# Attention and feed-forward on one core: loads held to 800 KB under way, pooled scores as four products on two banks, and a band mask built for one block and spread by VectorE

## The chip, the core and the metric

The kernel runs on one core of a Trainium2 chip. The metric is the device time of one execution in microseconds. Three timed runs of the kernel before gave 1001.52, 1004.47 and 1006.77 us, so its time is 1004.47 us (the median). The profile that is read here is of one more execution, which took 1000.71 us.

## What is computed

There are 8 batches, 8 heads, 576 tokens and a head size of 64. Each head runs two attentions over the same inputs, and their sum goes through a feed-forward layer:

```python
q_d = q.reshape(B, H, Sd, factor, D).mean(axis=3)      # k_d, v_d likewise; factor = 4, Sd = 144
out_up = np.repeat(sm_attn(q_d, k_d, v_d), factor, axis=2)
mask = np.abs(pos[:, None] - pos[None, :]) < factor
scores = np.where(mask, scale * np.matmul(q, k.transpose(0, 1, 3, 2)), -1000000000.0)
out_local = np.matmul(softmax(scores), v)
x = out_up + out_local                                  # tokens x 512
h = x @ w_in                                            # 512 -> 2048
out = (h * np.cos(h)) @ w_out                           # 2048 -> 512
```

The *pooled* attention works on 144 queries and 144 keys per head; the *local* one on a band of seven keys around each query.

## The kernel before

**Units.** The attention is cut into 32 units, one for each batch b and pair of heads. The two heads of a pair lie on partitions 0 to 63 and 64 to 127. A unit has these steps: `u_qk` loads q and k (292 KB each) and sums four neighbouring columns into `qkd`; `u_v` loads the value blocks `vl` (384 KB); `u_vd` loads (288 KB, batches 0 and 1 alone) and sums the pooled values, as `v_sum` does for the later batches; `u_s` makes the scores and the softmax of both attentions; `u_t` transposes the weights; `u_pv` multiplies by the values and writes x in two f16 parts.

**Local scores.** The 576 tokens are cut into 24 segments of 24 queries, each with 32 keys. Twelve blocks (`NBLK`) of 32 columns hold them: 48 products of 32x32 (L643) fill 384 columns of one PSUM bank `bl`. For batches 0 and 1 (`early`) the band mask is first put into the bank by a product of the bf16 identity with `mask_b` (L637), and VectorE takes the row maximum and subtracts it (L666, L667). Later batches add the f32 `mask` on VectorE (L670).

**Pooled scores.** The 144 queries of a head are cut into three overlapping groups of at most 64, so that the two heads stand on the two halves of the partitions: six products of 64 queries by 144 keys (L652) fill 432 columns of a second bank `bp`. VectorE takes the row maxima (L673), ScalarE the three exponentials (L681). The weights `smd` (128 x 3 x 144) are transposed in `u_t`, per half of the keys, by two transposes of 128 columns (L714) and one product of 32 columns (L716).

**Constants.** GpSimd builds the two identities, then the mask over all twelve blocks: a memset (L348), eight band selections of 32 partitions x 384 columns (L351, L353), four memsets for the edges (L356, L357) and a bf16 copy (L358).

**Feed-forward.** x is cut into 12 tiles of 384 tokens and the 2048 hidden columns into 16 chunks. One step, of 192, is `gemm1` (12 products of 128x384, L811), the evaluation of h cos h on ScalarE and VectorE, and `gemm2` (9 products of 128x512, L850). The first three tiles go through the chunks in blocks, while the weights are still arriving; later tiles take all 16 chunks at once. The weights come as 32 loads of 512 KB into a ring of seven buffers `wd`, which the loads of `u_vd` and `v_norm` share, and are split into f16 parts on VectorE and ScalarE (`w_split`). Partial results of the first three tiles are added in memory by GpSimd's transfers (L876); first parts and whole results are stored from SyncE's queue (L873).

**What sets the order.** All operations are recorded with an engine, a cost and their buffers in a `Plan`; `schedule` orders them by list scheduling over these costs, and the program is written out in that order, so each engine and SyncE's queue of transfers run it strictly in sequence. In gaps that the plan expects on TensorE in the first 300 us, filler products of the identity are put (L988), 16 of them ahead of the first unit. Loads of batches 0 and 1 and the weights are chained in one fixed sequence. Transfers from SyncE carry eight semaphores in turn, so that a ninth one waits for the first.

Of the kernel before, what the change touches and what calls it, by code (L numbers as in the profile page):

```python
# [12 lines left out]
F32 = mybir.dt.float32  # L13
I32 = mybir.dt.int32
BF16 = mybir.dt.bfloat16
F16 = mybir.dt.float16
AF = mybir.ActivationFunctionType
ALU = mybir.AluOpType
AX = mybir.AxisListType
# [5 lines left out]
P = 128  # L25
# [12 lines left out]
SD = S // 4  # L38
# [5 lines left out]
PAD = 3  # L44
SP_ = S + 8
NBLK = 2 * NSEG
QG = 64
NQG = -(-SD // QG)
F64_TOP = float(np.uint32(0x47EFFFFF).view(np.float32))
NEG = -2.0 ** 100  # L50
NEARLY = 2
# [2 lines left out]
GRP = 2  # L54
HOLD = 6
NWD = 7
EARLY = {0: dict(s="pa.0 pa.1 po.0 po.1", t="pa.2", v="ph.0 ph.1"),
         1: dict(s="pa.0 pa.1 po.0 po.1", t="pa.2 po.2", v="ph.0 ph.1 pa.0 pa.1 ph.0 ph.1 po.0 po.1")}
BOOST = {0: 100.0, 1: 30.0}
# [237 lines left out]
def _act(n, psum=True, extra=0):  # L297
    return n * 0.000833 + (0.051 if psum else 0.093) + 0.093 * extra


def _dve(n):
    return n * 0.001042 + 0.065
# [11 lines left out]
def attn_ffn_kernel(ctx: ExitStack, tc: tile.TileContext, qT, kT, vdn, vl, w_in, w_out, out):  # L314
# [21 lines left out]
    ident_b, ident = const.tile([P, P], BF16, name="ident_b"), const.tile([P, P], F32, name="ident")  # L336
    bquart, bhalf = const.tile([P, 1], F32, name="bquart"), const.tile([P, 1], F32, name="bhalf")
    ones, tiny = const.tile([P, P], F32, name="ones"), const.tile([P, P], F32, name="tiny")
    mask, mask_b = const.tile([P, NBLK, BS], F32, name="mask"), const.tile([P, NBLK, BS], BF16, name="mask_b")

    def constants():
        make_identity(nc, ident_b)
        make_identity(nc, ident)
        dve.memset(bquart, -0.25)
        dve.memset(bhalf, -0.5 * PI)
        dve.memset(ones, 1.0)
        dve.memset(tiny, TINY)
        pool.memset(mask, 0.0)  # L348
        for i in range(4):
            h = mask[i * BS:(i + 1) * BS]  # L350
            pool.affine_select(out=h, in_=h, compare_op=ALU.is_ge, fill=NEG, base=0,  # L351
                               pattern=[[0, NBLK], [1, BS]], channel_multiplier=-1)
            pool.affine_select(out=h, in_=h, compare_op=ALU.is_ge, fill=NEG, base=2 * PAD,  # L353
                               pattern=[[0, NBLK], [-1, BS]], channel_multiplier=1)
        for h in range(2):
            pool.memset(mask[2 * BS * h:2 * BS * h + BS, 0, 0:PAD], NEG)  # L356
            pool.memset(mask[2 * BS * h + BS:2 * BS * h + 2 * BS, NBLK - 1, BQ + PAD:BS], NEG)  # L357
        pool.tensor_copy(mask_b, mask)  # L358

# [13 lines left out]
    w_dram = {"i": w_in.bitcast(I32).rearrange("(a p) (f t) -> p a f t", p=P, t=2),  # L375
              "o": w_out.bitcast(I32).rearrange("f (n t) -> f n t", t=2)}

    loads = {}

    def dma(nbytes, fn, r=(), w=(), pw=()):  # L380
        o = pl.op("SP", max(0.45, nbytes / 262e3), fn, r=r, w=w, pw=pw, lat=1.8)
        loads.setdefault((pl.name,) + pl.arg, []).append(o)
        return o

# [168 lines left out]
    def bank(b, kind):  # L553

        if b < NEARLY:
            tags = EARLY[b][kind].split()
            return psum(tags[int(pl.turn(f"early{b}{kind}", len(tags)).split(".")[-1])])
        return psum(pl.turn("pa", 3))
# [63 lines left out]
    def u_s(b, pr):  # L622
        pl.name = "u_s"
        u = st[(b, pr)]
        q, k, qkd, qkg = u["q"], u["k"], u["qkd"], u["qkg"]
        early = b < NEARLY
        sml, smd = ub(b, pr, "sml"), ub(b, pr, "smd")
        bl, bp = bank(b, "s"), bank(b, "s")
        loc, poo = pl.buf(None), pl.buf(None)

        def using(bk, o):
            bk.r.append(o)
            bk.acc.append(o)

        def l_mm():
            if early:
                pe.matmul(bl.get()[:, :NBLK * BS], ident_b, mask_b.rearrange("p s n -> p (s n)"), start=True, stop=False)  # L637
            for a in range(NSEG // 2):
                for i in range(4):
                    for e in range(2):  # L640
                        for h in range(2):
                            hs, o, c, w = slice(64 * h, 64 * h + 64), (8 * a + 4 * e + i) * BQ, 4 * a + i, 2 * h + e
                            pe.matmul(bl.get()[BS * w:BS * (w + 1), BS * c:BS * (c + 1)], q.get()[hs, o:o + BS], k.get()[hs, o:o + BS],  # L643
                                      start=not early, stop=not early or c == NBLK - 1)
        if early:
            pl.op("PE", 1.2, l_mm, r=[q, k], pw=[bl], w=[loc])

        def d_mm():
            for g in range(NQG):
                for h in range(2):  # L650
                    hs, o = slice(64 * h, 64 * h + 64), min(g * QG, SD - QG)
                    pe.matmul(bp.get()[hs, g * SD:(g + 1) * SD], qkg()[hs, 0, o:o + QG], qkg()[hs, 1, :],  # L652
                              start=True, stop=True)
        if early:
            pl.op("PE", 0.6, d_mm, r=[qkd], pw=[bp], w=[poo])
        else:
            pl.op("PE", 1.5, lambda: (l_mm(), d_mm()), r=[q, k, qkd], pw=[bl, bp], w=[loc, poo])

        n, m = NBLK * BS, NQG * SD
        mxl, mxd, su = sb("mxl", 2, [P, NBLK]), sb("mxd", 2, [P, NQG]), sb("su", 2, [P, NBLK + NQG])  # L660
        sul, sud = lambda: su.get()[:, :NBLK], lambda: su.get()[:, NBLK:]
        lq = lambda: bl.get()[:, :n].rearrange("p (c n) -> p c n", n=BS)
        dq = lambda: bp.get()[:, :m].rearrange("p (g n) -> p g n", g=NQG)
        wide = lambda t, size: t.unsqueeze(2).broadcast_to([P, t.shape[1], size])
        if early:
            using(bl, pl.op("DVE", _dve(n), lambda: dve.tensor_reduce(out=mxl.get(), in_=lq(), axis=AX.X, op=ALU.max), r=[loc], w=[mxl]))  # L666
            using(bl, pl.op("DVE", _dve(n), lambda: dve.tensor_tensor(out=sml.get(), in0=lq(), in1=wide(mxl.get(), BS), op=ALU.subtract),  # L667
                            r=[loc, mxl], w=[sml]))
        else:
            using(bl, pl.op("DVE", _dve(n), lambda: dve.tensor_tensor(out=sml.get(), in0=lq(), in1=mask, op=ALU.add), r=[loc], w=[sml]))  # L670
            pl.op("DVE", _dve(n), lambda: dve.tensor_reduce(out=mxl.get(), in_=sml.get(), axis=AX.X, op=ALU.max), r=[sml], w=[mxl])
            sub(n, sml.get, sml.get, lambda: wide(mxl.get(), BS), r=[mxl], w=[sml])
        using(bp, pl.op("DVE", _dve(m), lambda: dve.tensor_reduce(out=mxd.get(), in_=dq(), axis=AX.X, op=ALU.max, negate=True),  # L673
                        r=[poo], w=[mxd]))
        part = pl.buf(None)

        def exps():
            act.activation(mxd.get(), mxd.get(), AF.Copy, scale=1.0 / 128.0)
            act.activation(sml.get(), sml.get(), AF.Exp, scale=0.125)
            for g in range(NQG):  # L680
                act.activation(smd.get()[:, g], dq()[:, g], AF.Exp, bias=mxd.get()[:, g:g + 1], scale=1.0 / 128.0,  # L681
                               accum_out=sud()[:, g:g + 1])
        using(bp, pl.op("ACT", _act(n, False) + 1.2, exps, r=[poo], w=[mxd, sml, smd], pw=[su, part], tab="exp"))
        pl.op("DVE", _dve(n), lambda: dve.tensor_reduce(out=sul(), in_=sml.get(), axis=AX.X, op=ALU.add), r=[sml], pw=[su, part])
        g = b // GRP
        pl.op("DVE", 0.1, lambda: dve.tensor_scalar(out=su.get(), in0=su.get(), scalar1=1e-9, scalar2=xnorm[g].get() if g else 2.0 * PI,
# [13 lines left out]
    def u_t(b, pr):  # L700
        pl.name = "u_t"
        u = st[(b, pr)]
        sml, smd = u["sml"], u["smd"]
        ptd = ub(b, pr, "ptd")
        pl.op("DVE", _dve(NBLK * BS), lambda: dve.transpose(sml.get().rearrange("p c n -> p (c n)"), sml.get().rearrange("p c n -> p (c n)")),
              w=[sml])
        for kh in range(2):
            bk = bank(b, "t")

            def t_mm(kh=kh, bk=bk):  # L710
                ks = slice(kh * HD, (kh + 1) * HD)
                to = bk.get()[:HD, :2 * SD].rearrange("p (h n) -> p h n", h=2)
                for g in range(NQG - 1):
                    pe.transpose(to[:, :, g * QG:(g + 1) * QG], smd.get()[:, g, ks], ident)  # L714
                w = SD - (NQG - 1) * QG
                pe.matmul(to[:, :, SD - w:], smd.get()[:, NQG - 1, ks], ident.rearrange("p (h n) -> p h n", h=2)[:, :, QG - w:],  # L716
                          start=True, stop=True)
            pl.op("PE", 4 * 0.065, t_mm, r=[smd], w=[bk])
            evac(2 * SD, lambda kh=kh: ptd.get()[:, kh],
                 lambda bk=bk: bk.get()[:HD, :2 * SD].rearrange("p (a n) -> p a n", a=2), bk, ptd, scale=1.0)  # L720
        u["ptd"] = ptd
# [26 lines left out]
    def u_pv(b, pr):  # L748
# [22 lines left out]
                            pe.matmul(banks[e].get()[64 * h:64 * h + 64, o:o + BQ], vt.get()[r, a, i, :], sml.get()[r, 4 * a + i, :BQ],  # L771
                                      start=True, stop=True)
        if b < NEARLY:
            pl.op("PE", 1.52, l_mm, r=[vt, sml], pw=banks, w=loc)
        else:
            pl.op("PE", 2.16, lambda: (d_mm(), l_mm()), r=[vd, ptd, vt, sml], pw=banks, w=loc + [poo])

        evac(SD, xd.get, lambda: banks[0].get()[:, 2 * SD:3 * SD], banks[0], xd, scale=0.25)
        xd.w[-1].deps += poo.w
# [194 lines left out]
                        best = (max(x[1], t0), x[1], x[2])  # L974
        return best

    last = CFG["f0"]
    with tc.manual_schedule():
        constants()
        for o in order:  # L980
            if o.eng == "PE" and o.start < CFG["fend"]:
# [5 lines left out]
                for _ in range(max(n, CFG["warm"][o.arg[0]] if early and s else 0)):  # L987
                    pe.matmul(s[2].get()[:, :2 * P], ident_b, ident_b.unsqueeze(1).broadcast_to([P, 2, P]), start=True, stop=True)  # L988
                last = o.start + o.dur
            o.fn()  # L990


def _lay(inputs):
# [32 lines left out]
```

## Time and profile before

| | us |
|---|---|
| median of three timed runs | 1004.47 (1001.52 to 1006.77) |
| profiled execution | 1000.71 |
| its span, first to last instruction | 998.9 |
| TensorE busy | 956.5 (96%) |
| VectorE busy | 649.1 (65%) |
| ScalarE busy | 601.2 (60%) |
| GpSimd busy | 220.2 (22%) |
| granted TensorE clock, mean | 0.981 |

A row of a group gives line, engine, operation, output and inputs by tile name, shapes, count, busy time and the mean duration. A row of the timeline gives start, duration, the instruction with its count, and in brackets the idle time of the engine before it with what ended it. f32 products appear as two records each, so that 48 products count as x96. PE is TensorE's products, PEld its weight loads, DVE VectorE, ACT ScalarE, POOL GpSimd, SP SyncE.

### The profile page before, as it was taken

To read this page: it belongs to the slowest core of one execution; us is meant where nothing else is said; L and a number is where in the kernel's file an instruction comes from. 1 tells how busy PE (TensorE), PEld (TensorE's weight loads), DVE (VectorE), ACT (ScalarE), POOL (GpSimd) and SP (SyncE) were. 2 spreads that over 40 slices of the span, in tenths; PEclk is the share of its full clock that TensorE was granted. 3 is DMA by queue.
4 is the path that set the end of the run, shared out by engine and by line. 5 is a ranking of instruction groups with operands and counts; after the bars stand their busy time and mean duration, and the time that the engine had idled before them with its cause. 6 is when DMAs were issued, how large, how long until landed. Compare 5 with 4: busy or idle time off the path is not lost.

```text
span 998.9 us, 26495 instructions
## 1 busy us (share of the span) xinstructions
PE 956.5 (96%) x11333; PEld 558.1 (56%) x11333; DVE 649.1 (65%) x1272; ACT 601.2 (60%) x1225; POOL 220.2 (22%) x360
## 2 busy tenths in 40 slices
PE   7788889989999999999999999999999999999998
PEld 5566445545556655655555665655555665555554
DVE  5968979697878856745555764755555764544443
ACT  2736667677887655656465764656555764644543
POOL 4544823241443311301011320401010210000000
PEclk8979979999999999999999999999999999999999
DMA  8632896576645631321100530321010000000000
GB/s 243 242 124 86 231 270 166 111 168 186 151 85 109 149 78 41 81 57 42 46 27 25 129 90 9 91 63 41 34 41 25 19 34 1 2 32 1 32 1 32
DMA packets 41854, 84.81 MB, mean 85 GB/s; under 512 B 4040, under 2 KB 14536, under 8 KB 41736
## 3 DMA queue, kind: packets, MB, share of 16 engines
q1 hardware_dynamic: 35256, 69.15, 21.6%
q0 software_dynamic: 6480, 13.96, 9.5%
q8 instruction: 89, 1.46, 0.6%
q14 instruction: 29, 0.24, 0.1%
HBM read 65.01 MB, written 18.09 MB: 83 GB/s over the span
## 4 chain that ended last, share of the span: by engine, by line
PE 81%; DVE 6%; ACT 3%; issue 3%; DMA 3%; POOL 2%; POOLq 0%; ACTq 0%; DVEq 0%
PE bank L850 33%; PE bank L811 33%; PE bank L771 4%; PE bank L643 3%; PE bank L652 3%; PE bank L759 2%; PE bank L988 1%; PE bank L714 1%; DMA out<-ob 1%; DMA wd<-vdn 1%; DVE wv L427 1%; DVE tr L826 1%; DVE wv L429 1%; DMA wd<-w_in 1%; ACT wd L435 1%
## 5 line engine op out<-in xcount | busy, mean ns | idle before, releaser
L850 PE MATMUL bank<-wo,gh 128*128 128x512 f16 x1152 | 343.9, 380 | 8.6 <-ACT ob L867 7.3
L811 PEld LDWEIGHTS <-wi 128*128 128x128 f16 x2304 | 225.5, 99 | 178.6 <-issue 12.8
L850 PE MATMUL bank<-wo,gl 128*128 128x512 f16 x576 | 218.6, 380 | 1.4 <-POOL gl L387 1.1
L825 ACT ACTIVATE tr<-bank,bquart,hs 128x384 int32<-128x384 f32 x192 | 128.3, 669 | 108.5 <-PE bank L811 102.8
L826 DVE SCALAR_TENSOR_TENSOR tr<-bank,hs,tr 128x384 f32<-128x384 f32 x192 | 117.9, 615 | 115.3 <-ACT tr L825 114.9
L850 PEld LDWEIGHTS <-gh 128*128 128x128 f16 x1152 | 109.5, 99 | 117.8 <-issue 15.4
L829 DVE SCALAR_TENSOR_TENSOR tr<-tr,rho,bank 128x384 f32<-128x384 f32 x192 | 116.8, 609 | 83.1 <-ACT tr L828 82.8
L828 ACT ACTIVATE tr<-tr,bhalf 128x384 f32<-128x384 f32 x192 | 117.4, 613 | 79.5 <-DVE tr L826 78.5
L831 ACT ACTIVATE gh<-tr 128x384 f16<-128x384 f32 x181 | 94.4, 521 | 113.5 <-DVE tr L829 113.2
L387 DVE TENSOR_TENSOR gl<-tr,gh 128x384 f16<-128x384 f32 x170 | 95.6, 563 | 67.5 <-ACT gh L831 66.2
L811 PE MATMUL bank<-x0h,wi 128*128 128x384 f16 x384 | 103.6, 332 | 7.4 <-DVE tr L829 5.2
L811 PE MATMUL bank<-x1h,wi 128*128 128x384 f16 x384 | 102.9, 330 | 0.0
L811 PE MATMUL bank<-x2h,wi 128*128 128x384 f16 x384 | 101.5, 326 | 0.7 <-DVE tr L829 0.7
L811 PE MATMUL bank<-x3h,wi 128*128 128x384 f16 x384 | 101.5, 326 | 0.0
L850 PEld LDWEIGHTS <-gl 128*128 128x128 f16 x576 | 56.5, 98 | 70.7 <-POOL gl L387 1.6
L574 POOL TENSOR_TENSOR qkd<-q 128x144 f32<-128x144 f32 x25 | 14.6, 585 | 264.6 <-PE bank L652 260.8
L811 PE MATMUL bank<-x0l,wi 128*128 128x384 f16 x192 | 63.8, 332 | 0.0
L811 PE MATMUL bank<-x1l,wi 128*128 128x384 f16 x192 | 63.4, 330 | 0.0
L811 PE MATMUL bank<-x3l,wi 128*128 128x384 f16 x192 | 62.6, 326 | 0.0
L811 PE MATMUL bank<-x2l,wi 128*128 128x384 f16 x192 | 62.6, 326 | 0.0
L771 PE MATMUL bank<-sml,vl 32*64 32x24 f32 x3072 | 53.0, 214 | 1.2 <-issue 0.7
L771 PEld LDWEIGHTS bank<-sml,vl 32*64 32x64 f32 x3072 | 49.4, 135 | 8.0 <-issue 5.2
(155 smaller groups left out, 1208.7 us busy)
## 6 DMA issues: line engine op xcount, KB each, us to landing
vl<-vl SPq DMA_DIRECT2D x32, 384.0 KB, 3.5
q<-qT SPq DMA_DIRECT2D x32, 292.0 KB, 3.7
k<-kT SPq DMA_DIRECT2D x32, 292.0 KB, 4.0
out<-ob SPq DMA_DIRECT2D x36, 256.0 KB, 2.7
out<-ob POOLq DMA_DIRECT2D x33, 256.0 KB, 5.8
wd<-w_in SPq DMA_DIRECT2D x16, 512.0 KB, 4.5
wd<-w_out SPq DMA_DIRECT2D x16, 512.0 KB, 6.3
wd<-vdn SPq DMA_DIRECT2D x18, 384.0 KB, 4.4
```

The costliest lines, as they stand in the source:

```text
L387: f = lambda e: lambda: e.tensor_tensor(out=out(), in0=in0(), in1=in1(), op=ALU.subtract)
L643: pe.matmul(bl.get()[BS * w:BS * (w + 1), BS * c:BS * (c + 1)], q.get()[hs, o:o + BS], k.get()[hs, o:o + BS], start=not early, stop=not ea ...
L652: pe.matmul(bp.get()[hs, g * SD:(g + 1) * SD], qkg()[hs, 0, o:o + QG], qkg()[hs, 1, :], start=True, stop=True)
L759: pe.matmul(banks[0].get()[64 * h:64 * h + 64, 2 * SD:3 * SD], vdg()[:, kh, 64 * h:64 * h + 64], ptd.get()[:, kh, h, :], start=(kh == 0), ...
L771: pe.matmul(banks[e].get()[64 * h:64 * h + 64, o:o + BQ], vt.get()[r, a, i, :], sml.get()[r, 4 * a + i, :BQ], start=True, stop=True)
L811: pe.matmul(ph.get()[:, :m], w[:, i, kc, :], x[:, kc, :], start=(n == 0), stop=(n == 3 * KC - 1))
L825: pl.op("ACT", _act(m, True, 2), lambda: act.activation(ti(), h(), AF.Identity, bias=bquart, scale=inv()), r=[ph, hs], w=[tr])
L826: pl.op("DVE", _dvs(m), lambda: dve.scalar_tensor_tensor(out=tr.get(), in0=h(), scalar=inv(), in1=ti(), op0=ALU.mult, op1=ALU.subtract), r ...
L828: pl.op("ACT", _act(m, False, 1), lambda: act.activation(tr.get(), tr.get(), AF.Sin, scale=2.0 * PI, bias=bhalf), w=[tr], tab="sin")
L829: pl.op("DVE", _dvs(m), lambda: dve.scalar_tensor_tensor(out=tr.get(), in0=tr.get(), scalar=rho(), in1=h(), op0=ALU.mult, op1=ALU.mult), r ...
L831: pl.op("ACT", _act(m, False), lambda: act.activation(gh.get(), tr.get(), AF.Copy), r=[tr], w=[gh], alts=[("DVE", _dve(m / 2), lambda: dve ...
L850: pe.matmul(o, (gh, gh, gl)[k].get()[:, sl], wo.get()[:, (0, 1, 0)[k]], start=(c == c0 and k == 0), stop=(c == c1 - 1 and k == 2))
```

## The change

**Loads.** Each transfer of SyncE that writes something is noted with its size. Ahead of each one the sizes of those before it are added up from the latest backwards; the first one that takes the sum over 800 KB must have landed. So three loads of 292 KB may be under way together, or two of 512 KB. Stores to `out` count too; GpSimd's transfers don't.

**Pooled scores.** Each head's first 128 queries are now one product of 64 rows x 128 columns, the two heads in different banks (L661), and the last 64 queries of both stand together as a third group (L664): four products of 144 columns in place of six. To fit, the blocks of the local scores are spread: blocks 0 to 7 lie in the first bank with the third group's place behind them, blocks 8 to 11 in the second behind two groups. What reads whole banks is cut in two: the mask product of early units, maximum and subtraction (or the mask's addition), and the pooled maxima. Both banks are held until the exponentials. In `u_t` the transposes take 96, 96 and 128 columns instead of 128, 128 and 32.

**Mask.** GpSimd builds `band` for one block of 32 columns, ahead of the identities; VectorE copies it, broadcast, into a bf16 `mask` for twelve blocks and sets the edges. There is no f32 mask any more.

The planner's costs of these steps change a little (`u_s` 1.2 to 1.31, 0.6 to 0.66, 1.5 to 1.62; `u_t` 0.26 to 0.29; `u_pv` 1.52 to 1.55, 2.16 to 2.22), and so does the order. The diff, cut:

```diff
-QG = 64
-NQG = -(-SD // QG)
+QG, HQ = 64, 48
+NQG = 3
+AHEAD = 800 << 10
...
     def constants():
+        pool.memset(band, 0.0)
+        for i in range(4):
+            h = band[i * BS:(i + 1) * BS]
+            pool.affine_select(out=h, in_=h, compare_op=ALU.is_ge, fill=NEG, base=0, pattern=[[1, BS]], channel_multiplier=-1)
+            pool.affine_select(out=h, in_=h, compare_op=ALU.is_ge, fill=NEG, base=2 * PAD, pattern=[[-1, BS]], channel_multiplier=1)
         make_identity(nc, ident_b)
+        dve.tensor_copy(mask, band.unsqueeze(1).broadcast_to([P, NBLK, BS]))
...
         make_identity(nc, ident)
...
-        pool.memset(mask, 0.0)
-        for i in range(4):
-            h = mask[i * BS:(i + 1) * BS]
...
-        pool.tensor_copy(mask_b, mask)
...
         o = pl.op("SP", max(0.45, nbytes / 262e3), fn, r=r, w=w, pw=pw, lat=1.8)
+        size[o] = nbytes if w else 0
...
+        lcut, gcut = ((0, 0, 8), (1, 2 * SD, NBLK)), ((1, 0, 2), (0, 8 * BS, NQG))
...
         def d_mm():
-            for g in range(NQG):
-                for h in range(2):
-                    hs, o = slice(64 * h, 64 * h + 64), min(g * QG, SD - QG)
-                    pe.matmul(bp.get()[hs, g * SD:(g + 1) * SD], qkg()[hs, 0, o:o + QG], qkg()[hs, 1, :],
-                              start=True, stop=True)
+            to = [t() for _, _, _, t in cuts(gcut, SD)]
+            for h in range(2):
+                hs = slice(64 * h, 64 * h + 64)
+                pe.matmul(to[h][:, 0], qkg()[hs, 0, :P], qkg()[hs, 1, :], start=True, stop=True)
+            for h in range(2):
+                hs = slice(64 * h, 64 * h + 64)
+                pe.matmul(to[0][hs, 1], qkg()[hs, 0, SD - QG:], qkg()[hs, 1, :], start=True, stop=True)
...
-                for g in range(NQG - 1):
-                    pe.transpose(to[:, :, g * QG:(g + 1) * QG], smd.get()[:, g, ks], ident)
-                w = SD - (NQG - 1) * QG
-                pe.matmul(to[:, :, SD - w:], smd.get()[:, NQG - 1, ks], ident.rearrange("p (h n) -> p h n", h=2)[:, :, QG - w:],
-                          start=True, stop=True)
+                for h in range(2):
+                    pe.transpose(to[:, h, :SD - HQ], smd.get()[:SD - HQ, 2 * h, ks], ident[:SD - HQ, :SD - HQ])
+                pe.transpose(to[:, :, SD - QG:], smd.get()[:, 1, ks], ident)
...
-            o.fn()
+            made = o.fn()
+            if size.get(o):
+                room = AHEAD
+                for prior, n in reversed(under):
+                    room -= n
+                    if room < 0:
+                        tc.add_manual_dep(made.ins, prior.name, sync, reason="bytes under way")
+                        break
+                under.append((made.ins, size[o]))
```

TensorE's sequence around the scores of the first unit (batch 0, pair 0), before and after; `ident_b` rows of L988 and L1006 are fillers:

```order
L637 LDWEIGHTS ident_b
L637 MATMUL bank<-mask_b,ident_b 128x384
L643 MATMUL bank<-k,q 32x32 x48
L988 LDWEIGHTS ident_b
L988 MATMUL bank<-ident_b 128x256
L652 MATMUL bank<-qkd 64x144 x6
```

```order
L647 LDWEIGHTS ident_b
L647 MATMUL bank<-mask,ident_b 128x256
L652 MATMUL bank<-k,q 32x32 x32
L647 LDWEIGHTS ident_b
L647 MATMUL bank<-mask,ident_b 128x128
L652 MATMUL bank<-k,q 32x32 x16
L1006 LDWEIGHTS ident_b
L1006 MATMUL bank<-ident_b 128x256
L661 MATMUL bank<-qkd 128x144 x2
L664 MATMUL bank<-qkd 64x144 x2
```

The mask product and the local products (L643, now L652) stand in two pieces, and the six pooled products have become two of 128x144 and two of 64x144. Later units have the same without mask rows and fillers.

VectorE's sequence where the softmax of the first unit is finished: `su` are the sums of the exponentials, `smd` the pooled weights, L605 and L606 the sums of pooled values of one unit, which set a `wd` buffer free. Before:

```order
L690 TENSOR_TENSOR smd<-smd,su 128x432
L686 TENSOR_SCALAR su<-su 128x15
L673 TENSOR_REDUCE mxd<-bank 128x3
L688 RECIPROCAL su<-su 128x15
L673 TENSOR_REDUCE mxd<-bank 128x3
L562 COPY ptd<-bank 72x288
L690 TENSOR_TENSOR sml<-sml,su 128x384
L690 TENSOR_TENSOR smd<-smd,su 128x432
L667 TENSOR_TENSOR sml<-bank,mxl 128x384
L705 STREAM_TRANSPOSE sml<-sml 128x384
L605 TENSOR_TENSOR wd<-wd 72x512
L606 TENSOR_TENSOR vd<-wd 72x256
```

And after:

```order
L679 TENSOR_TENSOR sml<-bank,mxl 128x256
L679 TENSOR_TENSOR sml<-bank,mxl 128x128
L688 TENSOR_REDUCE mxd<-bank 128x2
L688 TENSOR_REDUCE mxd<-bank 128x1
L605 TENSOR_TENSOR wd<-wd 72x512
L606 TENSOR_TENSOR vd<-wd 72x256
L703 TENSOR_REDUCE su<-sml 128x12
L705 TENSOR_SCALAR su<-su 128x15
L707 RECIPROCAL su<-su 128x15
L703 TENSOR_REDUCE su<-sml 128x12
L709 TENSOR_TENSOR smd<-smd,su 128x432
```

L605 and L606 moved from behind the scaling of two units' weights to a place ahead of the first unit's sums, and behind the maxima of two units alone.

## Prediction on record

> **What bounds the kernel now.** I read the page's head and chain first, then busy times by stage, then the timeline of the places that the change touches. The profiled execution took 1000.71 us, 1.8 us more than its span, and 3.8 us less than the median of the timed runs (1004.47). The sum below is made against the profiled one and carried over to the median as a difference.
>
> Span and chain from the page:
>
> ```profile
> span 998.9 us, 26495 instructions
> PE 81%; DVE 6%; ACT 3%; issue 3%; DMA 3%; POOL 2%; POOLq 0%; ACTq 0%; DVEq 0%
> ```
>
> Busy times by stage, with TensorE (PE) first, then its weight loads, VectorE, ScalarE, GpSimd, the granted clock, the share of the DMA engines and GB/s:
>
> ```profile
> 0.00:87.00 87.00, 69.66 (x1897) 52.14 (x1898) 64.53 (x145) 41.12 (x130) 35.93 (x62) 0.88 0.54 176
> 87.00:285.00 198.00, 177.41 (x1063) 96.77 (x1061) 163.50 (x330) 147.03 (x298) 80.32 (x146) 0.96 0.69 176
> 285.00:994.00 709.00, 709.00 (x8376) 409.20 (x8374) 420.51 (x799) 412.02 (x798) 103.96 (x152) 1.00 0.18 48
> ```
>
> There are three stages. Up to 87 us batches 0 and 1 go through attention alone, and no engine is full. Up to 285 us weights are split while the first tiles run, and TensorE is short of 20.6 us. From there on TensorE is busy without a gap at full clock, so that each tenth of a microsecond taken off a unit's products comes off the end, 24 times (batches 2 to 7), and work of VectorE or ScalarE costs nothing.
>
> **Part 1: pooled scores and transposes, 24 late units.** One unit of batch 2, in the timeline of TensorE:
>
> ```profile
> 285.91 1.02 PE L643 MATMUL bank<-k,q 64*32 64x32 f32 x96
> 286.87 0.95 PE L652 MATMUL bank<-qkd 64*64 64x144 f32 x12
> 287.75 0.60 PE L850 MATMUL bank<-wo,gh 128*128 128x512 f16 x2
> 289.15 0.71 PE L759 MATMUL bank<-ptd,vsum 72*64 72x144 f32 x8
> 289.79 1.59 PE L771 MATMUL bank<-sml,vl 32*64 32x24 f32 x96
> ```
>
> Six products of 144 columns take 287.75 - 286.87 = 0.88 us, the four of L759, with as many columns each, 289.79 - 289.15 = 0.64. Products run in pairs, one per half of the array, so one pair more costs 0.24 and a block of one shape has about 0.16 on top (0.88 - 3 x 0.24, and 0.64 - 2 x 0.24). That pairs run side by side is seen in windows so narrow that only the first records fall into them:
>
> ```profile
> 286.87 0.34 PE L652 MATMUL bank<-qkd 64*64 64x144 f32 x2
> 289.79 0.25 PE L771 MATMUL bank<-sml,vl 32*64 32x24 f32 x4
> ```
>
> The two of L652 go to one bank on different partitions. The four of L771 include pairs that differ in rows alone, write the same partitions and go to two banks (`banks[e]`): that is what the new wide pair (L661) does, so I count it as a pair. The new block is then two pairs of two shapes: 2 x (0.16 + 0.24) = 0.80, if each shape pays its own 0.16, which is 0.08 less than now; 0.64 and 0.24 less, if the second shape follows without it; 1.04 and 0.16 more, if the wide two run one after the other. I take 0.08, since each change of shape in these rows pays.
>
> The Trainium skill, TensorEngine Tiling (Array Packing), Key Properties, says that a change of tiling mode drains TensorE, and lists 64x128 and 64x64 as different modes; by that rule the saving is 0.08, without it 0.24. The same page, Restrictions and Gotchas, says that different row tiles can't use one PSUM bank at a time; by that the six products would have taken 6 x 0.24 + 0.16 = 1.60 us, where the trace has 0.88, so the measurement decides against it.
>
> The transposes, from a stretch where fillers (L988) follow at once:
>
> ```profile
> 83.28 0.38 PE L714 MATMUL bank<-ident,smd 128*72 128x128 f32 x2
> 83.50 0.26 PE L716 MATMUL bank<-ident,smd 128*72 128x32 f32 x2
> 83.59 0.27 PE L988 MATMUL bank<-ident_b 128*128 128x256 bf16 x1
> ```
>
> Two of 128 columns take 0.22, that is 0.11 each, and the product of 32 columns 0.09: 0.31. Now 96, 96 and 128 columns: 0.11 x 320 / 128 = 0.275, rounded to 0.04 less, twice per unit. So a late unit saves 0.08 + 0.08 = 0.16 us, and 24 units **3.8 us** (bounds: 24 x 0.32 = 7.7 saved, 24 x 0.16 = 3.8 lost when only the wide pair fails and the transposes gain nothing). Holding the first bank until the exponentials costs late units nothing: the next user of that bank is the unit's own second transpose, which needs the exponentials anyway.
>
> **Part 2: the mask.** GpSimd and TensorE at the start:
>
> ```profile
> 0.73 0.20 POOL masks.py:197 MEMSET ident_b<- 128x128 bf16 x1 [0.29 <-POOLq L1018]
> 1.01 0.29 POOL masks.py:199 TENSOR_SCALAR_AFFINE_SELECT ident_b<-ident_b 128x128 bf16<-128x128 bf16 x1
> 1.36 3.59 PE L988 MATMUL bank<-ident_b 128*128 128x256 bf16 x16 [1.36 <-POOL ident_b masks.py:199]
> 2.24 0.59 POOL L351 TENSOR_SCALAR_AFFINE_SELECT mask<-mask 32x384 f32<-32x384 f32 x1
> 2.90 0.58 POOL L353 TENSOR_SCALAR_AFFINE_SELECT mask<-mask 32x384 f32<-32x384 f32 x1
> 3.71 0.75 DVE L577 TENSOR_REDUCE qkd<-q 128x144 f32<-128x576 f32 x1 [2.51 <-DMA q<-qT]
> 4.45 0.76 DVE L577 TENSOR_REDUCE qkd<-k 128x144 f32<-128x576 f32 x1
> 8.46 0.32 PE L637 MATMUL bank<-mask_b,ident_b 128*128 128x384 bf16 x1 [3.51 <-POOL vq L471]
> ```
>
> q and k of the first unit are there by 4.45 at the latest, but the mask lets the first product go at 8.46. A selection takes 0.29 for 128 columns and 0.58 for 384, thus about 0.19 for 32, with 0.07 between two: eight take 2.1. With its memset (0.2 as for `ident_b`) the band is ready near 3.0, and `ident_b`, now behind it, another 1.01 + 0.29 - 0.73 = 0.57 later, near 3.6. VectorE's copy and memsets delay the first L577, for which I allow 0.8; the pooled scores that need it come after the local ones, and hide it. Late next are the 16 fillers, which wait for `ident_b`: 3.6 + 3.59 = 7.2. So the first product moves from 8.46 to 7.2: **1.3 us** (bounds 0, if a later wait swallows it, and 3.1, if the fillers take half their 3.59).
>
> **Part 3: what the earlier start lets move.** The order puts L605 and L606 of the first unit ahead of its sums. Now:
>
> ```profile
> 12.53 19.05 SPq L597 DMA_DIRECT2D wd<-vdn  x4
> SPq L597 <- DVE su L684: 14.7, 1, 14.7
> 29.10 0.80 DVE L605 TENSOR_TENSOR wd<-wd 72x512 f32<-72x512 f32 x1
> 36.48 0.42 SPq L570 DMA_DIRECT2D q<-qT  x1
> 52.52 0.48 PE L637 MATMUL bank<-mask_b,ident_b 128*128 128x384 bf16 x1
> 8.00:25.00 17.00, 14.56 (x460) 10.19 (x460) 10.41 (x20) 4.23 (x18) 4.77 (x8) 0.80 0.89 245
> 20.00:40.00 20.00, 15.81 (x398) 12.10 (x396) 19.86 (x42) 14.44 (x44) 10.31 (x9) 1.00 0.57 170
> ```
>
> The last `vdn` load waited 14.7 us for a buffer that L605/L606 free, and the first weights and batch 1's q and k (36.48) stand behind it in SyncE's queue. They will start earlier, but batch 1 begins (52.52) when TensorE is through with batch 0, so only what batch 0 itself saves counts. Up to 25 us VectorE is idle for 17 - 10.41 = 6.6 us, behind it (20 to 40) it is full and can't be moved. I take about half of the 6.6, **3.0 us** (bounds 0 and 6.6): loads arrive through these same microseconds.
>
> **Part 4: what the cuts cost in the eight early units.** Mean times by form:
>
> ```profile
> L666 DVE TENSOR_REDUCE mxl<-bank 128x12 f32<-128x384 f32 x8 | 4.4, 554 | 6.7 <-PE bank L643 6.7
> L501 DVE TENSOR_REDUCE vt<-bank 128x1 f32<-128x128 f32 x4 | 1.1, 283 | 0.0
> ```
>
> 271 ns for 256 columns leave 283 - 136 = 147 ns that an instruction takes whatever its size. Three more per unit, eight times, are 24 x 0.147 = 3.5 us of VectorE; I count a third, **1.2 us**, as on the path, since only 20 to 40 us is full (bounds 0 and 3.5). On TensorE the cut makes two more changes of shape, 2 x 0.16, and the unit saves 0.16 as above: 8 x 0.16 = 1.3, of which half, **0.6 us**, as TensorE is not full there (bounds 1.3 gained and 2.6 lost). The two further cuts of late units lie under a full TensorE.
>
> **Part 5: 800 KB under way.**
>
> ```profile
> 100.00:150.00 50.00, 42.12 (x209) 21.43 (x210) 43.33 (x84) 32.13 (x63) 27.03 (x47) 0.90 0.92 250
> q1 hardware_dynamic: 4970, 9.85, 59.4%
> wd<-w_out SPq DMA_DIRECT2D x4, 512.0 KB, 3.5
> out<-ob POOLq DMA_DIRECT2D x6, 256.0 KB, 7.4
> wd<-w_out SPq DMA_DIRECT2D x16, 512.0 KB, 6.3
> out<-ob POOLq DMA_DIRECT2D x33, 256.0 KB, 5.8
> ```
>
> The first four rows are of 100 to 150 us, the last two of the whole run; transfers end with the median time from issue to landing. SyncE's queue moved 9.85 MB there, 197 GB/s. Two loads of 512 KB (1.05 MB) that land in 3.5 us allow 300 GB/s, so the cap doesn't bind unless a landing takes over 1.05 / 0.197 = 5.3 us. What waits in SyncE instead of in the rings is served in the same sequence, and the stores behind it (L873) need `ob` anyway. I count **0** (bounds: 1.6 us gained, if GpSimd's additions (L876) come down here from 7.4 us to the run's 5.8; 9 lost as in rival D).
>
> Sum: -3.8 - 1.3 - 3.0 + 1.2 + 0.6 + 0 = -6.3 us. That is 994.4 for an execution like the profiled one, and 1004.47 - 6.3 = 998.2 for the median.
>
> **Rivals.**
> *B. The start does not reach the end* (-3.8 + 1.2 + 0.6 = -2.0 us, 1002.5). Parts 2 and 3 are eaten by waits that were hidden, such as L605 on VectorE waiting for its load, with the first units' sums queued behind it. For: TensorE is idle for 17.3 us up to 87, so its start alone does not set the pace. Against: VectorE has 6.6 us of idle there.
> *C. The clock follows the gaps* (-11.3, 993.2). 8 to 25 us ran at 0.80 and 100 to 150 at 0.90, which is 3.4 and 5.0 us of full clock lost, after stalls of TensorE. If the fillers run straight into the first unit and one later stall goes, about 5 us come on top. Against: a new gap elsewhere costs as much. The Trainium skill, TensorE: Matmul & The Clock Gate, Part 1, says that the clock halves after an idle window of about 3.4 us; the trace agrees, with 0.80 behind the idle 3.51.
> *D. Slower: the cap starves the stream* (+8, 1012). A landing includes the wait behind others, and over the whole run its median is 6.3 us; at that, two loads give 166 GB/s, and 9.85 MB take 59 us instead of 50. With 5 us of the same kind for batch 1's loads (from 36.48) that is 14 less 6. It decides from 5.3 us per 512 KB upwards. Against: the 6.3 contain the backlog that the cap removes.
> *E. The wide pair runs one after the other*: 3.8 lost instead of gained, -6.3 + 7.6 = 1.3 in all, 1005.8.
>
> **How the numbers follow.** 0.5%, 5 us, is about what a measurement of this kernel can tell from no change. The forecast has 0.45, of which 0.07 falls short of 5 us; B 0.24; C 0.14; D 0.12; E 0.05. Faster by over 0.5%: 0.38 + 0.14 = 0.52. Within: 0.07 + 0.24 + 0.05 = 0.36. Slower: 0.12. The range goes from 988, C with the larger bounds of parts 1 and 5 (993.2 - 3.9 - 1.6), to 1008, which leaves out most of D; the forecast's own is 994 to 1000, with the start's 4.3 us doubled or halved.
>
> **What would show it.** The first product of `gemm1` in the profile before:
>
> ```profile
> 86.73 0.34 PE L811 MATMUL bank<-x0h,wi 128*128 128x384 f16 x1
> ```
>
> It should start 2 to 3 us earlier, which is what parts 2 to 4 leave. L661 and L664 should take 0.80 from first start to the next line in a late unit (0.64 or 1.04 speak for the others); the first mask product should start near 7.2, and L605 before 20 us; TensorE stays full from about 283. The prediction is wrong if TensorE gets gaps after 285 us, or if 512 KB loads land in over 5.3 us and 100 to 150 us holds less of TensorE's work than now.

## The result, and the profile after

Twenty timed runs of each kernel gave 1000.66 us (median, 992.21 to 1004.20) after the change and 1009.36 us (1001.52 to 1019.19) before: a ratio of 0.992 with a 95% interval of 0.9898 to 0.9942, 6 to 10 us faster, where the prediction said 6.3. The time itself was forecast as 998.2 us with a range of 988 to 1008, and the measured 1000.66 lies inside it. The three runs of before that were known then (median 1004.47) were early ones of a wider spread, and the profiled execution of before (1000.71 us) lies below all twenty; that of after (1000.50) is an ordinary one. So the two spans, 998.9 and 998.7, hide the gain, and stretches have to be compared instead of sums.

Span and chain of after:

```profile
span 998.7 us, 26155 instructions
PE 78%; DVE 7%; DMA 5%; ACT 5%; issue 3%; POOL 1%; POOLq 0%; ACTq 0%; DVEq 0%; SPq 0%
```

The three stages of after, and the fifth and sixth row for two stretches inside the first (columns as before: length, TensorE, its weight loads, VectorE, ScalarE, GpSimd, granted clock, DMA share, GB/s):

```profile
0.00:87.00 87.00, 76.46 (x1782) 55.56 (x1785) 66.91 (x179) 40.33 (x126) 32.10 (x56) 0.77 0.59 176
87.00:285.00 198.00, 177.07 (x1206) 97.37 (x1203) 164.57 (x338) 145.67 (x296) 88.52 (x151) 0.95 0.70 177
285.00:994.00 709.00, 708.79 (x8155) 402.91 (x8153) 431.15 (x847) 414.08 (x809) 86.99 (x127) 1.00 0.19 48
...
40.00:52.00 12.00, 11.94 (x310) 9.54 (x305) 9.54 (x19) 6.64 (x16) 4.98 (x8) 0.50 0.89 267
74.00:94.00 20.00, 19.88 (x346) 14.88 (x346) 13.15 (x31) 6.46 (x18) 0.29 (x1) 0.50 0.18 54
```

In the chain TensorE has 78% where it had 81, and DMA 5% where it had 3. TensorE is full from 285 us as before. Up to 87 us it is busy 76.46 us where it was 69.66, but at a clock of 0.77 where it was 0.88. Busy time times clock, a rough measure, is 58.9 us where it was 61.3, so the start holds no more work than before but takes longer over it at the lower clock.

TensorE in after: the first unit, the first product of `gemm1`, the late transposes and a late unit's scores:

```profile
3.68 3.59 PE L1006 MATMUL bank<-ident_b 128*128 128x256 bf16 x16 [3.68 <-POOL ident_b masks.py:199]
7.06 0.42 PE L647 MATMUL bank<-mask,ident_b 128*128 128x256 bf16 x1
...
90.41 0.50 PE L828 MATMUL bank<-x0h,wi 128*128 128x384 f16 x1
...
296.56 0.33 PE L733 MATMUL bank<-ident,smd 96*72 96x96 f32 x2
296.73 0.27 PE L734 MATMUL bank<-ident,smd 128*72 128x128 f32 x1
296.84 0.59 PE L867 MATMUL bank<-wo,gh 128*128 128x512 f16 x2
...
298.51 1.02 PE L652 MATMUL bank<-k,q 64*32 64x32 f32 x96
299.46 0.52 PE L661 MATMUL bank<-qkd 64*128 64x144 f32 x4
299.91 0.46 PE L664 MATMUL bank<-qkd 64*64 64x144 f32 x4
300.30 0.34 PE L828 MATMUL bank<-x1h,wi 128*128 128x384 f16 x1
```

The first mask product starts at 7.06 (8.46 before). The pooled block takes 300.30 - 299.46 = 0.84 us, 0.45 for the wide pair and 0.39 for the other (0.88 before); the transposes take 0.28 (0.31 before). TensorE has 0.21 us of gaps from 285 to 994 us. But `gemm1` begins at 90.41, 3.7 us later than in the profile of before, where 2 to 3 us earlier was forecast.

### The profile page after: what moved, and what is told of

The parts are those of the page before. It is cut to its first block, busy times and chain, and to the rows that moved or that the text cites. A ratio compares the mean times of both kernels' runs of the same rounds, so it can differ in the third digit from the quotient of the medians.

```text
span 998.7 us, 26155 instructions
## 1 busy us (share of the span) xinstructions
PE 962.7 (96%) x11133; PEld 555.8 (56%) x11133; DVE 663.2 (66%) x1362; ACT 601.0 (60%) x1229; POOL 207.6 (21%) x334
## 3 DMA queue, kind: packets, MB, share of 16 engines
q8 instruction: 87, 1.43, 0.6%
## 4 chain that ended last, share of the span: by engine, by line
PE 78%; DVE 7%; DMA 5%; ACT 5%; issue 3%; POOL 1%; POOLq 0%; ACTq 0%; DVEq 0%; SPq 0%
PE bank L828 31%; PE bank L867 30%; PE bank L788 5%; PE bank L652 3%; PE bank L776 2%; PE bank L1006 2%; DMA wd<-w_in 2%; DMA wd<-vdn 2%; PE bank L661 1%; PE bank L664 1%; PE bank L733 1%; DVE tr L846 1%; DMA wd<-w_out 1%; ACT wd L477 1%; ACT tr L842 1%
## 5 line engine op out<-in xcount | busy, mean ns | idle before, releaser
L848 ACT ACTIVATE gh<-tr 128x384 f16<-128x384 f32 x173 | 90.1, 521 | 81.6 <-DVE tr L846 80.1
L828 PE MATMUL bank<-x3l,wi 128*128 128x384 f16 x192 | 62.6, 326 | 0.0
L828 PE MATMUL bank<-x2l,wi 128*128 128x384 f16 x192 | 62.6, 326 | 0.0
L709 POOL TENSOR_TENSOR sml<-sml,su 128x384 f32<-128x384 f32 x25 | 28.3, 1133 | 156.0 <-DVE su L707 145.8
L788 PE MATMUL bank<-sml,vl 32*64 32x24 f32 x3072 | 57.2, 222 | 1.7 <-issue 1.6
L788 PEld LDWEIGHTS bank<-sml,vl 32*64 32x64 f32 x3072 | 53.6, 146 | 9.2 <-issue 7.9
```

The lines of the kernel that those rows point to most:

```text
L709: f = lambda e, sm=sm, f=f, bc=bc: lambda: e.tensor_tensor(out=sm.get(), in0=sm.get(), in1=wide(f(), bc), op=ALU.mult)
L828: pe.matmul(ph.get()[:, :m], w[:, i, kc, :], x[:, kc, :], start=(n == 0), stop=(n == 3 * KC - 1))
L848: pl.op("ACT", _act(m, False), lambda: act.activation(gh.get(), tr.get(), AF.Copy), r=[tr], w=[gh], alts=[("DVE", _dve(m / 2), lambda: dve ...
```

## The experiments

Theory: the prediction's, that the earlier start and the late units make the gain, and the limit costs nothing. Rival: the limit makes it, since TensorE's waits put down to "issue" (waits for which the profile shows no cause) fell. Each ratio is to the kernel before, run on the same chip, with its 95% interval.

Profiles in one table, one execution each: the start of the first `gemm1` product, and how long groups of its 192 steps took, from first product to first product (us). Two profiles of one kernel differ by 9 us in the start (92.0 and 101.1 without the limit) and by little over 2 at most in the groups of steps:

| profile | first | steps 0-12 | 12-24 | 24-36 | 36-48 | 48-191 |
|---|---|---|---|---|---|---|
| before | 86.7 | 66.0 | 53.3 | 56.1 | 71.8 | 652.6 |
| before, mask alone | 91.6 | 62.6 | 52.1 | 56.3 | 72.1 | 652.6 |
| before, limit alone | 87.4 | 62.4 | 61.8 | 58.9 | 71.5 | 652.6 |
| order alone, 165 fillers | 90.7 | 59.2 | 57.3 | 51.5 | 70.9 | 650.5 |
| order alone, 158 fillers | 87.3 | 59.5 | 57.5 | 51.3 | 71.8 | 650.3 |
| order and late products | 84.6 | 59.9 | 57.1 | 51.0 | 71.5 | 648.3 |
| changed, no limit (two) | 92.0, 101.1 | 59.9, 59.7 | 57.1, 57.4 | 51.6, 51.1 | 70.2, 70.2 | 648.9, 649.7 |
| changed, no limit, 177 fillers | 88.7 | 60.9 | 56.2 | 51.0 | 70.4 | 648.3 |
| changed (two) | 90.4, 89.8 | 59.6, 60.2 | 65.0, 67.3 | 53.0, 52.4 | 70.2, 70.2 | 648.3, 648.2 |
| changed, 177 fillers | 77.7 | 62.9 | 64.2 | 51.8 | 70.4 | 648.3 |
| changed, 400 KB | 103.1 | 76.9 | 67.4 | 61.4 | 70.2 | 648.3 |

**The limit away** (e1_no_cap, and e8_no_cap beside e7_changed on a second chip).

```diff
-AHEAD = 800 << 10
+AHEAD = 800 << 20
```

> The changed kernel with the limit on bytes under way lifted (800 MB in place of 800 KB), everything else as changed. Theory of the prediction (the cap counts 0, the gain comes from the late units and from the start): the same time as the changed kernel, 8.7 us under the kernel before, a ratio of 0.991. Rival (the cap itself makes the gain, because TensorE's waits put down to issue fell from 9.7 us before to 3.1 us after in the first 300 us): about 6 us of the gain are lost, a ratio of 0.997, and TensorE's waits for issue are back at 7 us or more.

> The changed kernel itself, as the reference of this chip: a ratio of 0.992 to the kernel before.

> The changed kernel without the limit once more, now beside the changed kernel on one chip. Theory (the limit costs about 5 us, in the stretch from 100 to 215 us, where its profile held 237 GB/s against 301 from 120 to 150 us): 3 to 5 us under the changed kernel. Rival (the limit is free): the same time.

Measured: without the limit 0.9884 (0.9839 to 0.9929) and 0.9896 (0.9849 to 0.9944); the changed kernel beside the second 0.9929 (0.9900 to 0.9959), 1002.14 us against 997.56. The limit does not make the gain, which stands without it. By the medians the limit costs some 3 to 5 us, but the intervals overlap, so that the size is not shown. The rival's observation holds all the same. TensorE's waits up to 100 us, changed kernel first, then without the limit:

```profile
PE bank L788 <- issue: 1.6, 1, 1.6
PE bank L664 <- issue: 1.5, 1, 1.5
...
PE bank L652 <- issue: 0.2, 1, 0.2
```

```profile
PE bank L652 <- issue: 6.0, 3, 4.4
...
PE bank L664 <- issue: 3.2, 1, 3.2
```

With the limit such waits come to 3.3 us in the start, without it to 9.2; in the second profiles of the two it is 3.8 and 9.0. What the limit saves there it loses again where the weights stream. The changed kernel from 120 us, then the one without the limit:

```profile
120.00:150.00 30.00, 27.41 (x151) 14.79 (x150) 26.61 (x49) 20.34 (x41) 13.08 (x17) 1.00 0.93 237
150.00:215.00 65.00, 53.92 (x281) 28.30 (x281) 51.96 (x107) 47.73 (x101) 23.52 (x40) 0.92 0.73 190
```

```profile
120.00:150.00 30.00, 27.70 (x153) 14.91 (x152) 27.38 (x51) 22.04 (x44) 15.80 (x20) 1.00 1.04 301
150.00:215.00 65.00, 60.10 (x325) 32.47 (x324) 59.26 (x123) 54.78 (x115) 28.60 (x52) 0.97 0.74 195
```

237 GB/s in place of 301, and behind it TensorE holds 53.92 us of work in place of 60.10. The second profiles of the two kernels have 240 and 255 GB/s, so the throughput without the limit varies; TensorE's work is 53.41 and 61.09 us there, as in the first two. The place where it hurts, in the changed kernel: what SyncE's queue waited for from 140 to 156 us, its transfers up to a load of `vsum`, GpSimd's transfer that adds this one up, and TensorE:

```profile
SPq L410 <- DMA vl<-vl: 3.8, 1, 3.8
SPq L890 <- DMA wd<-w_in: 1.7, 1, 1.7
```

```profile
149.19 0.38 SPq L410 DMA_DIRECT2D wd<-w_in  x1
150.42 2.90 SPq L890 DMA_DIRECT2D out<-ob  x3
153.37 0.39 SPq L588 DMA_DIRECT2D vsum<-vdn  x1
```

```profile
157.74 0.88 POOL L590 DMA_DIRECT2D vsum<-vdn  x1 [10.90 <-DMA vsum<-vdn]
158.37 1.20 POOL L387 TENSOR_TENSOR gl<-tr,gh 128x384 f16<-128x384 f32 x1
```

```profile
159.62 0.61 PE L867 MATMUL bank<-wo,gl 128*128 128x512 f16 x1 [5.96 <-POOL gl L387]
```

And without the limit:

```profile
146.40 0.81 SPq L588 DMA_DIRECT2D vsum<-vdn  x1
```

```profile
153.28 0.88 POOL L590 DMA_DIRECT2D vsum<-vdn  x1 [4.47 <-DMA vsum<-vdn]
```

Without the limit SyncE's queue has no wait for a landing in this stretch. The load of 149.19 and the stores behind it wait for landings, which is the limit's wait for room, and the load of `vsum` behind them starts 7 us later (153.37 against 146.40). GpSimd waits 10.90 us for that load, with `gl` queued behind it, and TensorE waits 5.96 us for `gl`; without the limit TensorE has no such gap there. The wait for `gl` is 7.6 us in the second profile of the changed kernel and 4.8 in the one with 177 fillers, and stands in no profile of its order without the limit. In the table it is the column of steps 12 to 24: 64 to 67 us in all three profiles with the limit of 800 KB and the changed order, 56 to 58 in all six with this order and no limit.

**The limit tighter** (e6_cap_400: `AHEAD = 400 << 10`).

> The changed kernel with 400 KB in place of 800 KB, so that a load of 512 KB travels alone. Theory (the limit costs throughput where weights stream, from 100 to 215 us, and its cost grows as it gets tighter): 8 us or more over the changed kernel run beside it, with less than 237 GB/s from 120 to 150 us. Rival (the limit is free, or shorter landings pay for it): within 3 us of the changed kernel.

Measured: 1.0289 (1.0243 to 1.0334), 1038.05 us, 36 us over the changed kernel beside it. The same stretches:

```profile
120.00:150.00 30.00, 24.25 (x123) 12.19 (x122) 20.36 (x41) 19.00 (x37) 19.45 (x32) 0.97 0.81 187
150.00:215.00 65.00, 46.09 (x226) 23.80 (x226) 41.02 (x81) 34.10 (x67) 15.43 (x27) 0.83 0.61 174
```

187 GB/s in place of 237. Nothing but the limit was changed, so the cost is the limit's, and the throughput falls with it. It doesn't all lie in these stretches: the first `gemm1` product starts 13 us later, and steps 0 to 12 take 17 us more.

**The limit alone and the mask alone**, in the kernel before (e2_cap_alone adds `size`, `under` and the loop over them; e3_mask_alone takes `constants` of the changed kernel and `mask` for `mask_b` and the f32 mask).

> The kernel before with the limit of 800 KB alone. Theory of the prediction: no change, a ratio of 1.000, and TensorE's waits for issue stay near 9.7 us in the first 300 us. Rival (the cap makes the gain): about 6 us faster, 0.994, with TensorE's waits for issue at 4 us or less. A third view (the cap starves the stream): slower by 3 us or more, with the first loads of weights landing later.

Measured: 0.9995 (0.9960 to 1.0030). No change in sum, but not for the reason given: TensorE's issue waits fell from 10.4 us to 6.2 up to 100 us, and steps 12 to 24 took 61.8 us in place of 53.3. What the limit gives in return is not seen in this profile, which took 1008.98 us, 8 more than that of before, though the medians agree.

> The kernel before with the new mask alone (band on GpSimd, spread by VectorE, one bf16 mask). The plan does not know these instructions, so the order of everything else stays. Theory of the prediction: the first mask product starts at 7.2 in place of 8.46 us, and 1.3 us reach the end, a ratio of 0.9987. Rival: the start does not reach the end, 1.000.

Measured: 0.9982 (0.9947 to 1.0017), which tells 1.3 us neither from 0 nor from 4. The step itself is there:

```profile
7.07 0.53 PE L635 MATMUL bank<-mask,ident_b 128*128 128x384 bf16 x1
```

**Products and order without limit and mask** (e4_products_alone: `AHEAD` as in the first experiment, the old `constants`, `mask_b` for the early units).

> The changed kernel without the limit and with the old mask: the four pooled products, the cut reads and the changed order alone. Theory of the prediction: -3.8 (late units) -3.0 (loads earlier) +1.2 +0.6 = -5.0 us, a ratio of 0.995. Rival (the cap makes the gain): -3.8 + 1.8 = -2 us, 0.998.

Measured: 0.9891 (0.9851 to 0.9931). Either theory had less than half of it: the whole gain sits here. Against the first experiment, which has the new mask in place of the old (0.9884), the mask makes no difference that these runs show.

**The order alone** (e5_order_alone; e9_order_fewer_fillers). The kernel before with a table of the changed kernel's sequence, choice of engines and planned start times, from which the fillers are set too:

```diff
     order = pl.schedule()
+    place = {}
+    for i, k in enumerate(sorted(byk, key=repr)):
+        pos, e, t = struct.unpack_from("<HBf", raw, 7 * i)
...
+    order = sorted(pl.ops, key=lambda o: (place[o], o.i))
```

> The kernel before (six products, old mask, no limit), put into the order in which the changed kernel runs the same operations; an operation that the change cut in two stands where its last piece stood. Theory now (the new order makes most of the gain, since the limit alone gave 0.9995, the mask alone 0.9982 and products with order 0.9891): 7 to 9 us under the kernel before, a ratio of 0.992. Rival (the products make the gain): 1.000. The prediction's own part 3 with its bounds: 3 us, 0.997.

Measured: 0.9820 (0.9764 to 0.9875): the order alone is worth more than the whole change. More fillers are not the reason, since the kernel before has 173 and this one 165. Which part of it the choice of engines makes was not separated. Then seven fillers less, in one place near 9 us:

```diff
+                n = min(n, 2) if place[o] < 20 and n < 16 else n
```

> The kernel before in the changed kernel's order (as in the order-alone run), with 2 in place of 9 filler products ahead of the first unit's pooled scores, as the changed kernel has them there: 158 fillers in all in place of 165, the changed kernel 157. Theory (the four products and their cut reads in the early units cost what lies between order alone, 0.982, and the changed kernel without the limit, 0.989): the fillers don't matter, 0.982. Rival (the seven fillers keep the clock up): 0.989.

Measured: 0.9883 (0.9849 to 0.9916). The theory fell: with as many fillers as the changed kernel, old and new products read the same (0.9883 against 0.9884 and 0.9896). The early cuts need not cost anything, but a cost of 2 to 3 us, as large as what the late units save, would not show in intervals this wide. That the seven fillers make the rest is likely, but the two intervals overlap.

Where the order gains, by the table: 3 to 6 us in steps 0 to 12 and 5 in 24 to 36, with 4 to 5 given back between; not ahead of the first step. Steps 48 to 191 are 2 us shorter mainly because the scores of 18 late units fall into them in place of 19, which moves work and saves none. One place: the stretch 118 to 135 us and TensorE's gaps in it, two fences of before and then two of the order alone with 158 fillers:

```profile
118.00:135.00 17.00, 11.84 (x48) 5.42 (x46) 11.96 (x21) 8.34 (x17) 9.06 (x13) 0.70 1.04 274
```

```profile
123.88 0.59 PE L850 MATMUL bank<-wo,gh 128*128 128x512 f16 x2 [1.85 <-ACT ob L867]
126.75 1.01 PE L850 MATMUL bank<-wo,gh 128*128 128x512 f16 x2 [2.06 <-ACT ob L867]
129.43 1.01 PE L850 MATMUL bank<-wo,gh 128*128 128x512 f16 x2 [1.24 <-DVE ob L868]
```

```profile
118.00:135.00 17.00, 15.56 (x85) 8.13 (x83) 15.61 (x30) 11.29 (x21) 9.96 (x12) 1.00 1.08 282
```

```profile
123.80 0.59 PE L855 MATMUL bank<-wo,gh 128*128 128x512 f16 x2 [0.51 <-ACT ob L872]
125.53 0.59 PE L855 MATMUL bank<-wo,gh 128*128 128x512 f16 x2 [0.92 <-ACT ob L872]
```

Before, three results `ob` came while the additions of the last three were still landing. ScalarE and VectorE waited for these, from 115 to 136 us,

```profile
ACT ob L867 <- DMA out<-ob: 2.2, 1, 2.2
DVE ob L868 <- DMA out<-ob: 3.6, 1, 3.6
```

and TensorE waited 5.15 us for them, at a clock of 0.70. In GpSimd's queue the first additions stood at 115.50 and the next at 124.19 us; in the new order at 113.37 and 126.25. With more time between them the gaps are 1.43 us and the clock stays at 1.00. This one place is traced; the gain of steps 24 to 36 is not.

**The late units alone on that order** (e10_order_late).

```diff
     def u_s(b, pr):
+        if b < NEARLY:
+            return u_s_old(b, pr)
```

> The order-alone kernel with the four products and the new transposes in batches 2 to 7 alone; batches 0 and 1 keep the six products, the uncut reads and the old transposes; old mask, no limit. Theory (late units save 24 x 0.095 = 2.3 us, by first starts in the traces of before and after; what costs is the early units' cut): 0.980. Rival (the new products cost wherever they stand): 0.989. The prediction's own size for the late units, 3.8 us: 0.978.

Measured: 0.9829 (0.9792 to 0.9866), 988.69 us. It has 164 fillers, with those near 9 us among them, so order alone (0.9820) is the one to compare it with. The new products do no harm in late units that these runs show; the interval holds 0.980, and is too wide to size them. The table does: steps 48 to 191 take 650.3 to 650.5 us with the old products in this order and 648.3 with the new, 2.0 to 2.2 us for 18 units.

**More fillers** (e11_no_cap_fillers without the limit, e12_changed_fillers with it).

```diff
-           fgap=0.4, f0=0.8, fend=300.0, warm=(2, 1), fstep=0.13)
+           fgap=0.2, f0=0.8, fend=300.0, warm=(2, 1), fstep=0.11)
```

> The changed kernel without the limit, with 177 filler products in place of 157 (gap and step of the filler rule smaller, order unchanged). Theory of the clock (the granted clock was 0.961 to 0.977 in the runs of the changed kernel without the limit and 0.98 to 0.99 with order alone; the halved stretches follow from stalls of TensorE in the first 100 us, and fillers shorten them): a mean clock of 0.975 or more, and 4 us or more under the changed kernel without the limit, 0.985 or less. Rival (the clock follows waits that the plan does not foresee, so that fillers stand in the wrong places): 0.989 as without them.

> The changed kernel with its limit of 800 KB and with 177 filler products in place of 157. Theory (the limit costs throughput of loads, some 4.5 us between the two runs side by side, and fillers give some 6 us through the clock, each by itself): 0.983 + 0.0045 = 0.987, with a mean clock of 0.975 or more. Rival (the limit costs only through stalls that halve the clock, so that fillers take its cost away): 0.983. Second rival (the fillers gave nothing, and the run without the limit was better by its chip): 0.992, with a clock near 0.968.

Measured: 0.9827 (0.9792 to 0.9863) without the limit, 989.35 us, at mean clocks of 0.980 to 0.986; 0.9847 (0.9823 to 0.9871) with it, 992.06 us, at 0.979 to 0.987. Twenty fillers, 16 of them ahead of the first `gemm1` product, are worth some 8 us on the changed kernel, whose interval (0.9898 to 0.9942) lies wholly above. The change itself had lost 16 against the 173 of before, since the plan of the new order expects fewer gaps to fill. With 177 the first `gemm1` product starts 9 us earlier than in the profile of before:

```profile
77.71 0.34 PE L828 MATMUL bank<-x0h,wi 128*128 128x384 f16 x1
```

What the limit still costs beside more fillers, 0.002, is within the intervals. These two, order alone and order with the late products are faster than the changed kernel as well, with intervals apart from its own.

## Why the prediction was right, and where it was not

**The sum, -6.3, against about -8.7.** Its sign and size came out, out of terms that were off in both directions: order -11.7 (0.9883 on a kernel of 1003.95), late units -2.4, mask 0 to -1.8, limit +3 to +5. These add up to between -9 and -13, each with several us of uncertainty. That -6.3 came so near was in part luck: a gain of the order that was not foreseen and a cost of the limit that was put at nothing partly cancel.

**Part 1, late units: -3.8 predicted, -2.4 by the rows.** That the wide pair runs side by side, against rival E, and each shape pays its own change was right: 0.84 where 0.80 was counted, so 0.04 saved and not 0.08. The transposes save 0.03 and not 0.04. 24 x (0.04 + 2 x 0.03) = 2.4 us, 0.10 a unit, and the 18 units in the table agree with 0.11 to 0.12. The mis-sized term is the fixed part per shape (0.16 counted, (0.45 + 0.39) / 2 - 0.24 = 0.18 measured), which the block pays twice. For the transposes a saving of 0.035 was rounded up to 0.04.

**Part 2, mask:** the first product at 7.2 predicted, 7.06 measured. Whether it reaches the end stays open.

**Part 3, the start: the step that failed.** L605 went early as said:

```profile
14.98 0.68 DVE L605 TENSOR_TENSOR wd<-wd 72x512 f32<-72x512 f32 x1
```

It stood at 29.10. But the prediction let the order act on the first 90 us alone, "so only what batch 0 itself saves counts", and said `gemm1` would begin 2 to 3 us sooner. Without added fillers, and the limit of 400 KB aside, it began at 84.6 to 101.1 us in the new order, against 86.7 to 91.6 in the old, with no gain that these profiles agree on. Rival B had said so of the start. But the order's gain came later, between 87 and 262 us, for which neither the prediction nor B had counted anything.

**Part 4:** the cut maxima of the early units,

```profile
L677 DVE TENSOR_REDUCE mxl<-bank 128x8 f32<-128x256 f32 x8 | 3.3, 418 | 8.2 <-PE bank L661 8.1
L677 DVE TENSOR_REDUCE mxl<-bank 128x4 f32<-128x128 f32 x8 | 2.2, 279 | 0.0
```

take 5.5 us where they took 4.4: 1.1 more, against 8 x 0.147 = 1.2. With the subtractions and the pooled maxima it is 16.7 in place of 13.6, 3.1 more against 3.5 counted. What of it reaches the end was not seen.

**Part 5 and rival D, the limit: 0 predicted, +3 to +5 by the medians.** The failed step is "what waits in SyncE instead of in the rings is served in the same sequence": the loads are, but stores and the `vsum` load stand behind them in the same queue, and GpSimd's `gl` behind those. D's price for the stream (9 us) is near that of the table (8 to 10 in steps 12 to 24), but by luck, since its mechanism and its place were others: loads of 512 KB were to land in over 5.3 us, and 100 to 150 us was to lose. In the changed kernel TensorE holds 44.79 us of work from 100 to 150, where it held 42.12, and in its second profile the median landing of the `w_out` loads there is put at 3.6 us; over the whole run with 177 fillers it is 3.9, and 4.4 for `w_in`. The loss comes from 150 to 215 us, 53.92 in place of 59.34, from what stands behind the held loads. D also missed that the waits at the start shrink.

**Rival C, the clock.** The clock moves the time by as much as a term of the sum, but the change did not bring a gain of it. Twenty more fillers raised the mean clock from 0.967 to about 0.981 and took 8 us off, where C had put 5. The changed kernel's mean clock was 0.967 (median of twenty), that of before 0.973 (median of the 54 runs beside the experiments that the comparisons use); beside each other on one chip it was 0.969 and 0.9715. Over those 54 runs, a straight line through times and clocks gives 7 us per 0.01. This is a correlation, since a stall takes time of its own too; by it the change lost an estimated 2 to 4 us. Nor does the order gain through the clock: without the limit the changed kernel was 0.9884 of before at a mean clock of 0.973, where before had 0.972 on the same chip.

The prediction saw the clock of 0.80 behind an idle of 3.51 us of TensorE. In the changed kernel the two longest halved stretches, 36.3 to 60.2 and 73.9 to 94.3 us, come behind much shorter idles:

```profile
36.32 0.80 PE L497 MATMUL bank<-ident,vm 128*128 128x128 f32 x2 [1.31 <-DVE vm L494]
72.02 0.53 PE L788 MATMUL bank<-sml,vl 32*64 32x24 f32 x19 [1.57 <-issue]
```

## What to carry to other kernels

A change to a planner's costs is a change to the whole order: compare stage by stage to the end of the last stage that is not full, and run the order by itself. A limit on bytes under way, put into a queue that also carries stores and small loads, delays these too: ask who waits for what stands behind the held transfer. And where the clock differs between runs, compare mean clocks before comparing times, and count the fillers that a new order leaves.

## What the hardware showed that was not expected

The clock halves for whole stretches (0.50) while TensorE is busy: 11.94 of 12 us from 40 to 52 and 19.88 of 20 from 74 to 94 in the changed kernel, in rows shown above. The Trainium skill, TensorE: Matmul & The Clock Gate, Part 1, has the clock come back after one busy window of about 3.4 us; these two rows don't agree with it, unless products on a part of the array don't count as busy. Both stretches mix these with fillers on the whole array, which are 7.2 us of TensorE's busy time from 36.5 to 60. No run here separates the two. Nor was it settled what TensorE's "issue" waits are. In the changed kernel they come to 9.2 and 9.0 us up to 100 us without a limit and to 3.3 and 3.8 with 800 KB under way, but to 6.0 with 400 KB.
